# A sliding-window decode layer on one core: its loads on two DMA queues, SyncE's and ScalarE's, and issued one step ahead of use

## The chip, the core and the metric

The kernel runs on one core of a Trainium2 chip. The core has a matrix engine (TensorE, PE in the profile, with weight loads as PEld), a vector engine (VectorE, DVE), a scalar engine (ScalarE, ACT), GpSimd (POOL) and SyncE (SP), which does no arithmetic and here issues DMAs. Sixteen DMA engines move data between HBM and the core's SBUF. Each engine runs its own instructions in program order; engines wait for each other through semaphores. A DMA is issued by an instruction of SP, ACT or POOL and goes into the issuing engine's own queue; an issue that must wait for a buffer holds back what stands behind it on that engine.

The metric is the device time of one execution in microseconds (us), as a median over runs.

## The reference

For two sequences with one new token each, the layer normalises x, and adds to x an attention over a window of the cache and a gated feed-forward part, both computed from the normalised xn. All data are float32.

```python
xn = layernorm(x)                                 # x: (2, 1, 512)
# attention: 32 query heads, 8 key heads, head size 128, the last W = 4096 of 32768 keys
q = (xn @ wq).reshape(2, 1, 32, 128)              # wq: (512, 4096)
k = repeat(k_cache[:, :, Sk - W:, :], 4, axis=1)  # four query heads share a key head
v = repeat(v_cache[:, :, Sk - W:, :], 4, axis=1)
p = softmax(q . k * 128 ** -0.5)
attn = (p . v).reshape(2, 1, 4096) @ wo           # wo: (4096, 512)
# feed-forward: F = 1792
gate = xn @ W_gate
up = xn @ W_up
glu = ((gate * (gate > 0)) * up) @ W_down
return x + attn + glu
```

Each input element is used once or for four heads, so the work is mostly that of bringing 94.9 MB from HBM into SBUF.

## The kernel before, in words

**Groups and tiles.** The 2 x 8 pairs of sequence and key head are cut into four groups g of four key heads of one sequence (`g` = 2r + b, with r the half of the heads and b the sequence). A group's keys come as two tiles, a = 0 and 1, of two heads each, its values likewise. `load_kv` (line 85) loads such a tile: 128 partitions x 8192 floats, 4096 KB, with 32 KB in a row per partition. In this document k(g,a) and v(g,a) are these tiles.

**The ring.** All large loads go through one pool of four buffers, `ring` (`RING = 4`): in this order wq in two halves (`load_wq`, line 75), w_gate and w_up (`load_ff`, line 79), k(0,0), k(0,1), then k(1,0), v(0,0), k(1,1), v(0,1), and so on, a tile of K of group g and one of V of group g-1 in turn up to k(3,1), v(2,1), then v(3,0), v(3,1), w_down (`load_down`, line 82) and wo in two halves, wo0 and wo1, the second in five pieces (line 434). The n-th tile takes the buffer of tile n-4, so its load waits until that tile's last reader is done: a K tile is freed by DVE's second transpose of it, a V tile by PE's last product with it, a weight by PE's last product. All these loads are issued by SP (`nc.sync.dma_start`, line 71) in the order above. The small x is loaded from ACT's queue (line 105).

**The order of the work** is written out by hand (`manual_schedule`): each engine runs its instructions in the order in which the program names them.

- Start: the statistics of x, xn and its transpose; q = xn @ wq into `q_ps` (line 195), 64 matmuls, of which the first 32 read the first half of wq; then `load_ff` twice; the transposes of q (`qt`) and copies of it into `qz` by DVE and ACT (line 217); then `g_ps` and `u_ps` (line 225) from w_gate and w_up, and h.
- `keys(g, a, ...)` (line 242): for each half of the tile, DVE transposes it (line 249, `kT`) and PE adds 16 products to the scores `s` (line 254). After either half it runs a list of `steps`, work of the group before that is put there by hand.
- `softmax(g)` (line 263): maxima on DVE and PE, then the exponentials on ACT (line 286). `turn(g)` (line 290): DVE transposes the result and copies it into `pts` (lines 292, 298).
- `values(g, a, v)` (line 310): 32 matmuls of `pts` with the V tile (line 317).
- `join(g, a)` (line 366): `mask` on DVE (line 326) and `gather` on PE (line 337), after a = 1 also the sums. `close(g)` (line 372): `finish` on DVE, and after each second group `spread_heads` (line 352), PE products whose result ACT copies into `oT` (line 360).

The loop over groups runs like this, with the joins of group g-1 put into the steps of the following `keys`:

```python
for g in range(1, NG):
    for a in range(NP):
        kt_in = load_kv(k_cache, "k", g, a)
        v_in = load_kv(v_cache, "v", g - 1, a)
        keys(g, a, kt_in, steps)
        if a:
            softmax(g)
        values(g - 1, a, v_in)
        if a:
            turn(g)
```

At the end come `values` and `join` of group 3, the product of h with w_down, `spread_heads(1)`, and the products of `oT` with wo (line 415, `yw_ps`; the last four chunks at line 419), one copy each by ACT and DVE and the store of the result.

Of the kernel before, what the change touches and what calls it, by code (L numbers as in the profile page):

```python
# [20 lines left out]
def kernel(  # L21
# [12 lines left out]
    nc = tc.nc  # L34
    P = 128
    B, _, D = x.shape
    _, HKV, SK, DH = k_cache.shape
    HQ = wq.shape[1] // DH
    REP = HQ // HKV
    F = w_gate.shape[1]  # L40
    W = min(4096, max(256, SK // 4))
    KC = D // P
# [6 lines left out]
    NG = B * R  # L49
    S1 = W // (Q * 512)  # L50

    NP = C // 2
# [13 lines left out]
    ctx.enter_context(tc.manual_schedule())  # L66


    def load(name, src, shape):
        t = ring.tile(shape, F32, name=name, tag="ring")  # L70
        nc.sync.dma_start(t, src)
        return t


    def load_wq(m):
        src = wq[m * 2 * P:(m + 1) * 2 * P, :].rearrange("(p k) f -> p k f", p=P)
        return load(f"wq{m}", src, [P, 2, HQ * DH])

    def load_ff(w, name):
        return load(name, w.rearrange("(p k) f -> p k f", p=P), [P, KC, F])  # L80

    def load_down():
        return load("wd", w_down.rearrange("(p k) e -> p k e", p=P), [P, FB, D])

    def load_kv(cache, name, g, a):
        r, b = divmod(g, B)
        base = cache[b, r * C + 2 * a, SK - W:SK, :]
        run = J * DH
        src = bass.AP(
            tensor=cache.tensor, offset=base.offset, ap=[[run, PK], [SK * DH, 2], [1, run]]  # L90
        )
        return load(f"{name}{g}_{a}", src, [P, run])


    NJ = HQ * DH // (R * P)
# [8 lines left out]
    x2 = const.tile([B, D], F32, name="x2")  # L104
    nc.scalar.dma_start(x2, x[:, 0, :])
    wqt = [load_wq(m) for m in range(2)]

    ident = const.tile([P, P], F32, name="ident")
# [68 lines left out]
    for kc in range(KC):  # L177
        m, k = divmod(kc, 2)
# [12 lines left out]
    for kc in range(KC):  # L191
        for r in range(R):
            for c in range(C):
# [2 lines left out]
                    q_ps[r][32 * c:32 * c + 32, :], xnT[:, 0, kc, :], wqt[kc // 2][:, kc % 2, n * 512:(n + 1) * 512],  # L196
                    start=(kc == 0), stop=(kc == KC - 1),
                )
    gw = load_ff(w_gate, "wg")
    uw = load_ff(w_up, "wu")  # L200
    for r in range(R):
        qs = work.tile([P, 512], F32, name=f"qs{r}", tag="qs")
        (nc.vector.tensor_copy if r else nc.scalar.copy)(qs, q_ps[r])  # L203
# [5 lines left out]
        for m in range(NB):  # L209
            src = qt[32 * m:32 * m + 32, :, :, 0].rearrange("p i (t h) b -> p b t h i", h=2)  # L210
# [31 lines left out]
    def keys(g, a, kt_in, steps=((), ())):  # L242

        if a == 0:
            ss[g] = ps_s.tile([P, 512], F32, name=f"s{g}", tag="s")
        for mh in range(2):
            kt = ktp.tile([P, J, 2, 32], F32, name=f"kT{g}_{a}_{mh}", tag="kT")
            src = kt_in.rearrange("p (j d) -> p j d", d=DH)[:, :, PK * mh:PK * mh + PK]
            nc.vector.transpose(kt.rearrange("p j m i -> p j (m i)"), src)  # L249
            for m in range(2):  # L250
                for h in range(2):
                    for s1 in range(S1):
                        q = 2 * h + s1
                        nc.tensor.matmul(  # L254
                            ss[g][32 * q:32 * q + 32, :], qz[:, g, 2 * mh + m, a, h], kt[:, JS * s1:JS * s1 + JS, m, h::2],
                            start=(a == 0 and mh == 0 and m == 0), stop=(a == NP - 1 and mh == 1 and m == 1),
                        )
            for step in steps[mh]:
                step()
# [3 lines left out]
    def softmax(g):  # L263

        m = work.tile([P, 1], F32, name=f"m{g}", tag="m")
        nc.vector.tensor_reduce(out=m, in_=ss[g], op=ALU.max, axis=AX.X)  # L266
        mt = ps_1.tile([1, P], F32, name=f"mt{g}", tag="misc")
        nc.tensor.transpose(mt, m, ident)
        mx = work.tile([1, 2, TK], F32, name=f"mx{g}", tag="mx")
        nc.vector.tensor_reduce(  # L270
            out=mx, in_=mt.rearrange("p (h x k) -> p h k x", h=2, k=TK), op=ALU.max, axis=AX.X
        )
        mb = work.tile([1, 2, S1 * Q, TK], F32, name=f"mb{g}", tag="mb")
        nc.vector.tensor_scalar(
            mb, mx[:, :, None, :].to_broadcast([1, 2, S1 * Q, TK]), -SCALE, None, op0=ALU.mult
        )
        nm_ps = ps_1.tile([P, 1], F32, name=f"nm_ps{g}", tag="misc")
        nc.tensor.matmul(nm_ps, mb.rearrange("p h x k -> p (h x k)"), ones, start=True, stop=True)
        nm = work.tile([P, 1], F32, name=f"nm{g}", tag="nm")
        nc.vector.tensor_copy(nm, nm_ps)  # L280

        l = ls[g] = work.tile([P, 1], F32, name=f"l{g}", tag="l")
        pv = pz.rearrange("p j (i h) -> p j i h", h=2)
        for h in range(2):
            o = slice(PK * h, PK * h + PK)
            nc.scalar.activation(  # L286
                pv[o, :, :, h], ss[g][o].rearrange("p (j i) -> p j i", j=JS), AF.Exp, bias=nm[o], scale=SCALE, accum_out=l[o],
            )

    def turn(g):  # L290
        pT = work.tile([P, JS, Q, NP, REP], F32, name=f"pT{g}", tag="pT", bufs=1)
        nc.vector.transpose(pT.rearrange("p j x t k -> p (j x t k)"), pz.rearrange("p j s -> p (j s)"))  # L292
        pts[g] = work.tile([P, NP, S1, JS, 2, REP], F32, name=f"pt{g}", tag="pt")
        for h in range(2):
            for s1 in range(S1):
                q = 32 * (2 * h + s1)
                for x in range(Q):
                    nc.vector.tensor_copy(  # L298
                        pts[g][32 * x:32 * x + 32, :, s1, :, h], pT[q:q + 32, :, x].rearrange("p j t k -> p t j k")
                    )  # L300
# [3 lines left out]
    def total(g):  # L304
        lps[g] = ps_1.tile([HR, 1], F32, name=f"lp{g}", tag="misc")
        nc.tensor.matmul(lps[g], by_h.rearrange("p t h k -> p (t h k)"), ls[g], start=True, stop=True)
# [3 lines left out]
    def values(g, a, v):  # L310
        o = os[a] = ps_1.tile([P, 512], F32, name=f"o{g}_{a}", tag=f"o{a}")
        for s1 in range(S1):
            for jh in range(2):
                for q in range(Q):
                    j = 16 * jh + 4 * q
                    lo = (JS * s1 + j) * P
                    nc.tensor.matmul(  # L317
                        o[32 * q:32 * q + 32, :],
                        pts[g][:, a, s1, j:j + 4].rearrange("p u h k -> p (u h k)"), v[:, lo:lo + 512],
                        start=(s1 == 0 and jh == 0), stop=(s1 == S1 - 1 and jh == 1),  # L320
                    )

    def mask(g, a):
        o = os[a]
        ons[a] = work.tile([P, 4, P], F32, name=f"on{g}_{a}", tag="on")
        nc.vector.tensor_tensor(  # L326
            ons[a], o.rearrange("p (u d) -> p u d", u=4), own_u[:, :, None].to_broadcast([P, 4, P]), op=ALU.mult
        )
# [4 lines left out]
    def gather(g, a):  # L333

        if a == 0:
            oa[g] = ps_1.tile([HR, 4, P], F32, name=f"oa{g}", tag="oa")
        nc.tensor.matmul(  # L337
            oa[g].rearrange("h u d -> h (u d)"), pick[:, 8 - 8 * a:24 - 8 * a],
            ons[a].rearrange("p u d -> p (u d)"), start=(a == 0), stop=(a == NP - 1),
        )  # L340
# [11 lines left out]
    def spread_heads(r):  # L352
# [6 lines left out]
            )  # L359
        nc.scalar.copy(oT[:, r], op)  # L360

    for a in range(NP):
        keys(0, a, load_kv(k_cache, "k", 0, a))
    softmax(0)
    turn(0)
    def join(g, a):
        mask(g, a)
        gather(g, a)
        if a:
            total(g)  # L370

    def close(g):
        finish(g)
        if g % B == B - 1:
            spread_heads(g // B)

    steps = ((), ())
    for g in range(1, NG):
        for a in range(NP):
            kt_in = load_kv(k_cache, "k", g, a)  # L380
            v_in = load_kv(v_cache, "v", g - 1, a)
            keys(g, a, kt_in, steps)
            if a:
                softmax(g)
            values(g - 1, a, v_in)
            if a:
                turn(g)
            steps = (
                (lambda g=g, a=a: join(g - 1, a),), (lambda g=g: close(g - 1),) if a else (),
            )  # L390
    for step in steps[0] + steps[1]:
        step()
    g = NG - 1
    vin = [load_kv(v_cache, "v", g, a) for a in range(NP)]
    dw = load_down()


# [25 lines left out]
    for a in range(NP):  # L423
        values(g, a, vin[a])
        join(g, a)
# [52 lines left out]
```

## Time and profile before

| | us |
|---|---|
| median of 3 runs | 230.38 |
| lowest and highest run | 230.38 and 230.39 |
| the profiled execution, its own time | 230.5 |
| its span (first to last instruction) | 228.5 |
| PE busy | 132.5 |
| DVE busy | 118.6 |
| ACT busy | 14.2 |

Times in the profile count from the start of the span. A line of a timeline gives the start, the length, the engine, the line of the kernel, the operation, out<-in by the tiles' names, the shapes and, after an x, how many instructions it merges; in square brackets stands the idle time of the engine ahead of it and who ended that. A line of the chain of waits gives a start, a length and who was at work. SPq and ACTq are the issues of DMAs; names leave out the numbers of tiles, so that which K tile a row means follows from the order. The row of digits called DMA cuts the span into 40 equal slices and gives the busy share of the 16 DMA engines in tenths.

### The profile page before, as it was taken

Reading aid. Unit: us, or ns where it says so; the run is one execution under the profiler, and the core shown is the slowest. Engines: PE = TensorE matmul, PEld = TensorE weight load, DVE = VectorE, ACT = ScalarE, POOL = GpSimd, SP = SyncE. Lnnn points to the kernel's source line nnn. Section 1 sums busy time; section 2 is a strip of 40 time slices with the busy share of each in tenths; the row PEclk is TensorE's granted clock in tenths of the full one; section 3 lists DMA queues with packets and bytes.
Section 4 is the critical chain, followed back from the end, with each engine's and each line's share of the span. In section 5 each row is a group of like instructions: output and inputs, shape, how many; then the busy total and the mean of one; then the engine's idle time right before and its main releaser. Section 6 shows DMA issues by size and latency. Waiting matters only on the chain.

```text
span 228.5 us, 2062 instructions
## 1 busy us (share of the span) xinstructions
PE 132.5 (58%) x864; PEld 38.7 (17%) x864; DVE 118.6 (52%) x160; ACT 14.2 (6%) x40; POOL 3.7 (2%) x11
## 2 busy tenths in 40 slices
PE   0584929603636005876906975508928735989693
PEld 0521203101001001211201311102401201223211
DVE  2300032319893399972599893799179295012000
ACT  2000022000000400000200000200000200000001
POOL 6000000000000000000000000000000000000000
PEclk9999575985897655897775899956997995599679
DMA  7999999999999999999999999999999999999991
GB/s 276 459 402 418 467 412 416 453 459 401 430 453 424 403 453 453 393 436 459 419 413 453 433 396 453 445 419 424 453 413 419 453 439 389 461 446 410 412 380 38
DMA packets 3916, 95.03 MB, mean 416 GB/s; under 512 B 442, under 2 KB 450, under 8 KB 836
## 3 DMA queue, kind: packets, MB, share of 16 engines
q1 hardware_dynamic: 3896, 94.90, 97.0%
q8 instruction: 7, 0.11, 0.2%
q10 hardware_dynamic: 12, 0.01, 0.0%
q14 instruction: 1, 0.01, 0.0%
HBM read 94.90 MB, written 0.00 MB: 415 GB/s over the span
## 4 chain that ended last, share of the span: by engine, by line
DMA 60%; DVE 20%; PE 14%; issue 3%; ACT 2%; SPq 0%; DVEq 0%; ACTq 0%
DMA k<-in_A_k_cache_dram 37%; DVE kT L249 15%; DMA wo<-in_A_wo_dram 13%; DMA wq<-in_A_wq_dram 9%; PE yw_ps L415 4%; PE s L254 3%; PE o L317 3%; PE q_ps L195 3%; DVE pt L298 2%; DVE on L326 1%; ACT pz L286 1%; DVE m L266 1%; ACT L286 1%; DVE pT L292 1%; PE y_ps L419 0%
## 5 line engine op out<-in xcount | busy, mean ns | idle before, releaser
L254 PE MATMUL s<-kT,qz 128*32 128x512 f32 x256 | 44.2, 815 | 58.4 <-DVE kT L249 58.4
L249 DVE STREAM_TRANSPOSE kT<-k 128x4096 f32<-128x4096 f32 x16 | 70.6, 4429 | 12.8 <-DMA k<-in_A_k_cache_dram 12.8
L317 PE MATMUL o<-v,pt 128*32 128x512 f32 x256 | 34.5, 672 | 0.0
L254 PEld LDWEIGHTS s<-kT,qz 128*32 128x32 f32 x256 | 8.7, 128 | 86.8 <-issue 61.9
L298 DVE COPY pt<-pT 32x256 f32<-32x256 f32 x64 | 18.2, 285 | 1.0
L195 PE MATMUL q_ps<-wq,xnT 128*32 128x512 f32 x64 | 12.9, 980 | 4.3 <-DMA wq<-in_A_wq_dram 4.3
L217 DVE COPY qz<-qt 32x32 f32<-32x32 f32 x16 | 3.0, 188 | 22.5 <-ACT qz L217 22.5
L337 PE MATMUL oa<-on,pick 128*16 128x512 f32 x16 | 10.1, 721 | 6.9 <-DVE on L326 6.9
L317 PEld LDWEIGHTS o<-v,pt 128*32 128x32 f32 x256 | 9.4, 121 | 19.4 <-issue 19.3
L326 DVE TENSOR_TENSOR on<-o,own_u 128x512 f32<-128x512 f32 x8 | 5.4, 672 | 12.8 <-PE o L317 12.8
L286 ACT ACTIVATE pz<-s,nm 64x512 f32<-64x512 f32 x8 | 5.8, 731 | 80.7 <-DVE nm L280 80.6
L415 PE MATMUL yw_ps<-wo,oT 128*2 128x512 f32 x56 | 8.6, 783 | 2.2 <-DMA wo<-in_A_wo_dram 2.2
L292 DVE STREAM_TRANSPOSE pT<-pz 128x1024 f32<-128x1024 f32 x4 | 5.0, 1245 | 8.3 <-ACT pz L286 8.3
L446 DVE COPY yo<-y_ps 128x128 f32<-128x128 f32 x1 | 0.3, 292 | 16.9 <-PE y_ps L419 16.9
L266 DVE TENSOR_REDUCE m<-s 128x1 f32<-128x512 f32 x4 | 2.8, 692 | 11.5 <-PE s L254 11.5
L183 PE MATMUL xt_ps<-rep,xc 2*128 2x32 f32 x16 | 3.7, 402 | 8.4 <-DVE rep L176 8.4
L195 PEld LDWEIGHTS q_ps<-wq,xnT 128*32 128x32 f32 x64 | 3.0, 168 | 13.1 <-issue 7.7
L225 PE MATMUL g_ps<-wg,xnT 128*32 128x448 f32 x32 | 5.0, 791 | 0.0
L183 PEld LDWEIGHTS xt_ps<-rep,xc 2*128 2x128 f32 x16 | 3.6, 319 | 8.4 <-DVE rep L176 8.4
L206 PE MATMUL qt<-ident,qs 128*128 128x128 f32 x8 | 1.7, 357 | 4.4 <-DVE qs L203 4.4
L337 PEld LDWEIGHTS oa<-on,pick 128*16 128x16 f32 x16 | 1.6, 113 | 15.2 <-DVE on L326 9.8
L355 PEld LDWEIGHTS op<-osb,spread 16*128 16x128 f32 x32 | 3.7, 186 | 1.8 <-issue 1.8
(68 smaller groups left out, 53.9 us busy)
## 6 DMA issues: line engine op xcount, KB each, us to landing
k<-in_A_k_cache_dram SPq DMA_DIRECT2D x8, 4096.0 KB, 29.4
v<-in_A_v_cache_dram SPq DMA_DIRECT2D x8, 4096.0 KB, 28.5
wq<-in_A_wq_dram SPq DMA_DIRECT2D x2, 4096.0 KB, 16.8
wo<-in_A_wo_dram SPq DMA_DIRECT2D x1, 4096.0 KB, 30.1
wg<-in_B_W_gate_dram SPq DMA_DIRECT2D x1, 3584.0 KB, 29.5
wu<-in_B_W_up_dram SPq DMA_DIRECT2D x1, 3584.0 KB
wd<-in_B_W_down_dram SPq DMA_DIRECT2D x1, 3584.0 KB
wo<-in_A_wo_dram SPq DMA_DIRECT2D x1, 2048.0 KB, 19.5
```

What stands on the lines that cost most here:

```text
L183: nc.tensor.matmul(xt_ps[:, v, kc, :], lhsT, rep16.rearrange("r s b -> r (s b)"), start=True, stop=True)
L195: nc.tensor.matmul(q_ps[r][32 * c:32 * c + 32, :], xnT[:, 0, kc, :], wqt[kc // 2][:, kc % 2, n * 512:(n + 1) * 512], start=(kc == 0), stop ...
L249: nc.vector.transpose(kt.rearrange("p j m i -> p j (m i)"), src)
L254: nc.tensor.matmul(ss[g][32 * q:32 * q + 32, :], qz[:, g, 2 * mh + m, a, h], kt[:, JS * s1:JS * s1 + JS, m, h::2], start=(a == 0 and mh == ...
L266: nc.vector.tensor_reduce(out=m, in_=ss[g], op=ALU.max, axis=AX.X)
L286: nc.scalar.activation(pv[o, :, :, h], ss[g][o].rearrange("p (j i) -> p j i", j=JS), AF.Exp, bias=nm[o], scale=SCALE, accum_out=l[o],)
L292: nc.vector.transpose(pT.rearrange("p j x t k -> p (j x t k)"), pz.rearrange("p j s -> p (j s)"))
L298: nc.vector.tensor_copy(pts[g][32 * x:32 * x + 32, :, s1, :, h], pT[q:q + 32, :, x].rearrange("p j t k -> p t j k"))
L317: nc.tensor.matmul(o[32 * q:32 * q + 32, :], pts[g][:, a, s1, j:j + 4].rearrange("p u h k -> p (u h k)"), v[:, lo:lo + 512], start=(s1 == ...
L326: nc.vector.tensor_tensor(ons[a], o.rearrange("p (u d) -> p u d", u=4), own_u[:, :, None].to_broadcast([P, 4, P]), op=ALU.mult)
L337: nc.tensor.matmul(oa[g].rearrange("h u d -> h (u d)"), pick[:, 8 - 8 * a:24 - 8 * a], ons[a].rearrange("p u d -> p (u d)"), start=(a == 0 ...
L415: nc.tensor.matmul(yw_ps[32 * c:32 * c + B, :], lhsT, w, start=(n < Q), stop=(n >= wide - Q))
```

## The change

Loads get a queue. SP keeps the first half of wq, w_gate, all K tiles, v(3,0), v(3,1), w_down and wo. ACT gets the second half of wq, w_up and the V tiles of groups 0, 1 and 2. The loop now issues the tiles of the next step after it has named the keys of this one, so that the issues on ACT stand at given places among its other work: v(0,0) ahead of softmax(0), v(g-1,1) after keys(g,0), v(g,0) ahead of softmax(g). The order in which tiles take the ring's buffers is as before.

```diff
-    def load(name, src, shape):
+    def load(name, src, shape, queue=nc.sync):
         t = ring.tile(shape, F32, name=name, tag="ring")
-        nc.sync.dma_start(t, src)
+        queue.dma_start(t, src)
         return t
...
-        return load(f"wq{m}", src, [P, 2, HQ * DH])
+        return load(f"wq{m}", src, [P, 2, HQ * DH], nc.scalar if m else nc.sync)
...
-    gw = load_ff(w_gate, "wg")
-    uw = load_ff(w_up, "wu")
+    gw = load_ff(w_gate, "wg", nc.sync)
+    uw = load_ff(w_up, "wu", nc.scalar)
...
+    def load_k(g, a):
+        return load_kv(k_cache, "k", g, a)
+
+    def load_v(g, a):
+        return load_kv(v_cache, "v", g, a, nc.scalar if g < NG - 1 else nc.sync)
+
     for a in range(NP):
-        keys(0, a, load_kv(k_cache, "k", 0, a))
+        kt_in = load_k(0, a)
+        keys(0, a, kt_in)
+    k_next = load_k(1, 0)
+    v_next = load_v(0, 0)
     softmax(0)
     turn(0)
...
     for g in range(1, NG):
         for a in range(NP):
-            kt_in = load_kv(k_cache, "k", g, a)
-            v_in = load_kv(v_cache, "v", g - 1, a)
+            kt_in, v_in = k_next, v_next
             keys(g, a, kt_in, steps)
-            if a:
+            if a == 0:
+                k_next = load_k(g, 1)
+                v_next = load_v(g - 1, 1)
+            else:
+                if g < NG - 1:
+                    k_next = load_k(g + 1, 0)
+                v_next = load_v(g, 0)
                 softmax(g)
             values(g - 1, a, v_in)
...
-    vin = [load_kv(v_cache, "v", g, a) for a in range(NP)]
+    vin = [v_next, load_v(g, 1)]
     dw = load_down()
```

More of the change, by code (lines that the diff above doesn't have):

```diff
@@ L76, in load_wq, with load_ff, load_kv @@
         src = wq[m * 2 * P:(m + 1) * 2 * P, :].rearrange("(p k) f -> p k f", p=P)
-        return load(f"wq{m}", src, [P, 2, HQ * DH])
-    def load_ff(w, name):
-        return load(name, w.rearrange("(p k) f -> p k f", p=P), [P, KC, F])
+        return load(f"wq{m}", src, [P, 2, HQ * DH], nc.scalar if m else nc.sync)
+    def load_ff(w, name, queue):
+        return load(name, w.rearrange("(p k) f -> p k f", p=P), [P, KC, F], queue)
     def load_down():
         return load("wd", w_down.rearrange("(p k) e -> p k e", p=P), [P, FB, D])
-    def load_kv(cache, name, g, a):
+    def load_kv(cache, name, g, a, queue=nc.sync):
         r, b = divmod(g, B)
@@ L91, in load_kv @@
         )
-        return load(f"{name}{g}_{a}", src, [P, run])
+        return load(f"{name}{g}_{a}", src, [P, run], queue)
     NJ = HQ * DH // (R * P)
```

## The prediction

> **What bounds the kernel now.** I read the page first, then the chain of waits, then the timelines of SP, DVE, ACT and PE. A tile of group g and pair a is written k(g,a) or v(g,a).
>
> ```profile
> span 228.5 us, 2062 instructions
> ...
> DMA  7999999999999999999999999999999999999991
> ...
> q1 hardware_dynamic: 3896, 94.90, 97.0%
> ```
>
> One queue moves 94.90 MB, its packets fill 97.0% of the span on the 16 DMA engines, and the busy digit is 9 in every slice but the first and the last. The transfers are the bound; compute matters only where it frees a ring buffer too late. The chain of waits in order of time gives the pace:
>
> ```profile
> 29.35 30.88 DMA k<-in_A_k_cache_dram
> ...
> 103.67 24.96 DMA k<-in_A_k_cache_dram
> ...
> 138.06 29.27 DMA k<-in_A_k_cache_dram
> ...
> 184.72 30.11 DMA wo<-in_A_wo_dram
> ```
>
> A row starts at an issue or at the last wait before it, and ends at the landing: k(0,1) at 60.23, k(2,1) at 128.63, k(3,1) at 167.33, wo0 at 214.83. k(3,1), issued at 138.06, took 29.27 us: three tiles are in flight at a time. From the first to the second there are seven tiles, k(1,0), v(0,0), k(1,1), v(0,1), k(2,0), v(1,0), k(2,1): 68.40 / 7 = 9.77 us each (a tile is 128 x 8192 x 4 bytes, 4.194 MB). The next four take 38.70 / 4 = 9.68. The stream runs without a hole from 60 to 215, so v(0,1), fourth after k(0,1), landed at about 60.23 + 4 x 9.77 = 99.3.
>
> How near is a hole? The timeline of SP's issues:
>
> ```profile
> 44.12 0.54 SPq L71 DMA_DIRECT2D v<-in_A_v_cache_dram  x1
> ...
> 92.67 0.53 SPq L71 DMA_DIRECT2D k<-in_A_k_cache_dram  x1
> 98.59 0.54 SPq L71 DMA_DIRECT2D v<-in_A_v_cache_dram  x1
> ...
> 145.93 0.54 SPq L71 DMA_DIRECT2D v<-in_A_v_cache_dram  x1
> ...
> 159.74 8.19 SPq L71 DMA_DIRECT2D v<-in_A_v_cache_dram  x2
> ```
>
> These are v(0,0) at 44.12, k(2,0) at 92.67, v(1,0) at 98.59, then v(2,1) at 145.93, and v(3,0) and v(3,1) from 159.74 on, the second at 167.4. At 92.67 only v(0,1) is still in flight, with 6.6 us left. This is the thinnest place of the stream. How long a transfer takes that starts into an empty queue is shown by the tile view of wq:
>
> ```profile
> DMA to landing us min/median/max: 12.2/16.8/21.4
> ```
>
> The first wq half needs 12.2 us where a tile in the flow needs 9.77, so an issue must come some 2.4 us before the flow runs dry. The margin at k(2,0) is therefore 6.6 - 2.4 = 4.2 us.
>
> **The change part by part.** Bytes, tiles, the order of the ring's four buffers and which reader frees which buffer stay the same; "one step ahead" alters program order only, and SP already issued a tile as soon as its buffer was free. The eight issues that leave SP save it eight times about 0.5 us that the stream covers: nothing. ACT gets them; an issue of 0.54 us there lies in an engine that is idle for tens of us between softmaxes. A waiting issue holds back what stands behind it on ACT: v(g,0) stands ahead of the exponentials of group g and waits for values(g-1,0), but on PE those end before keys(g,1), on which the exponentials wait anyway. Nothing there. Two other effects do cost.
>
> First: two transfers of different queues are now in flight together, and nothing orders them. At the start wq0 and wq1 share the engines and land together, and so do w_gate and w_up. The timelines of PE and DVE:
>
> ```profile
> 13.09 6.27 PE L195 MATMUL q_ps<-wq,xnT 128*32 128x512 f32 x32 [1.02 <-DMA wq<-in_A_wq_dram]
> 22.68 6.60 PE L195 MATMUL q_ps<-wq,xnT 128*32 128x512 f32 x32 [3.32 <-DMA wq<-in_A_wq_dram]
> ...
> 35.23 5.02 PE L225 MATMUL g_ps<-wg,xnT 128*32 128x448 f32 x32
> 40.84 3.21 PE L225 MATMUL u_ps<-wu,xnT 128*32 128x448 f32 x32 [0.58 <-DMA wu<-in_B_W_up_dram]
> ...
> 181.02 3.64 PE L317 MATMUL o<-v,pt 128*32 128x512 f32 x32
> ...
> 214.87 8.63 PE L415 MATMUL yw_ps<-wo,oT 128*2 128x512 f32 x56 [2.23 <-DMA wo<-in_A_wo_dram]
> ```
>
> ```profile
> 50.54 8.77 DVE L249 STREAM_TRANSPOSE kT<-k 128x4096 f32<-128x4096 f32 x2 [4.83 <-DMA k<-in_A_k_cache_dram]
> 60.35 8.77 DVE L249 STREAM_TRANSPOSE kT<-k 128x4096 f32<-128x4096 f32 x2 [1.04 <-DMA k<-in_A_k_cache_dram]
> ...
> 167.35 4.45 DVE L249 STREAM_TRANSPOSE kT<-k 128x4096 f32<-128x4096 f32 x1 [6.71 <-DMA k<-in_A_k_cache_dram]
> ...
> 189.13 0.69 DVE L326 TENSOR_TENSOR on<-o,own_u 128x512 f32<-128x512 f32 x1
> ```
>
> The first half of q's products, hidden under the second half's load so far, now starts only when both have landed, at 22.7. All 64 end at 22.7 + 6.3 + 6.6 = 35.6, 6.3 later. The steps from there to g_ps keep their 5.9 us: g_ps at 41.5, u_ps at 46.5, its end at 49.7. w_gate and w_up are there by then (15.7 MB, 40.8 as before), and k(0,0) and k(0,1), issued at about 29 and 36, wait behind them: no hole, k(0,0) at 50.5 as before. But v(0,0) goes out at 49.7 beside k(0,1), where one queue had put it two tiles behind. Its flow starts, in terms of landings, at 49.7 + 2.4 = 52.1; k(0,1) would land at 60.2 and has 8.1 us to go. If the two share equally, these take twice as long: **k(0,1) lands 8.1 us later**, at 68.3. Bounds: nothing if SP's queue is served first, 9.77 if all of v(0,0) goes first. The trace of before has no two large transfers on two queues, so I take the middle, equal shares, as both consist of the same packets.
>
> The Trainium skill, "DMA: Bandwidth & Descriptors", section "Queues, rings and completion order", says that each DMA engine serves its queues in turn, a packet at a time; by it the 8.1 would stand. No run so far shows it.
>
> DVE is idle ahead of both pairs of transposes, so keys(0,1), softmax(0), keys(1,0) and with them the issue of k(2,0) move by the same 8.1, to 100.8. v(0,1) also goes out later, as on ACT it stands behind the exponentials of group 0, but k(1,0) and k(1,1), issued long before, cover it.
>
> The stream, whose bytes are the same, still runs dry at 99.3 with v(0,1). Delay less margin: 8.1 - 4.2 = **a hole of 3.9 us**. A byte lost there is not made up, so everything in the stream moves by 3.9: wo0 from 214.83 to 218.7. Later issues move by 8.1 against a flow later by 3.9, and there the margins hold. The nearest is k(2,1): k(2,0) issued at 100.8 has about 4 us left when v(1,0) joins it at 109.1; sharing brings k(2,0) in at 117, v(1,0) at 129 and k(2,1) at 136.4, and DVE, which by the chain of waits took it as it landed, comes to it at 128.63 + 8.1 = 136.7. At k(3,1) DVE had waited 6.71 us. There compute catches up: k(3,1) lands at 171.2, and DVE, ready at 168.7, is from then on 3.9 late, not 8.1.
>
> Second: v(2,1). ACT's timeline has the copy that now stands ahead of it, and the last one of its kind:
>
> ```profile
> 163.80 0.18 ACT L360 COPY oT<-op 128x32 f32<-128x32 f32 x1 [19.56 <-PE op L355]
> ...
> 212.68 0.18 ACT L360 COPY oT<-op 128x32 f32<-128x32 f32 x1 [29.65 <-PE op L355]
> ```
>
> Its buffer is free at 145.93, but on ACT it stands behind the copy of oT, which ends at 163.98, 172.1 with the delay. So v(2,1), until now ahead of v(3,0), comes behind it or beside it. v(3,0) is out at 167.8 and alone would land at 181.0; v(2,1) joins at 174.5, so both run at half pace until v(3,0) lands at 187.5; the 3.3 us left of v(2,1) take 6.6 beside v(3,1): 194.1. values(2,1), 3.64 us in the row at 181.02, ends at 197.7; the mask behind it, at 189.13 before, is **8.6 late**, and so is all of PE's work for group 3 up to the last oT copy. That copy had been done at 212.86, 2.0 ahead of wo0; now 221.4, 2.7 behind it. The last projection starts at 221.4 instead of 214.87, 6.6 later.
>
> Some of this comes back: wo1's pieces are then there, and the 56 matmuls that took 8.63 ran at 3.12 for 24 where nothing held them:
>
> ```profile
> 219.09 3.12 PE L415 MATMUL yw_ps<-wo,oT 128*2 128x512 f32 x24
> ```
>
> That is 7.3 for 56, 1.3 less. So +6.6 at most, +3.9 (the stream) at least. I take 6.6 - 1.3 = +5.3: 230.5 of the profiled execution (its span is 228.5) becomes 235.8. The median of the runs is 0.1 below the profiled execution: **235.7 us**.
>
> **The rivals.**
>
> *No hole* (22%). If the engines serve the queues in the order of issue, or SP's first, k(0,1) is not late by more than the 4.2 margin and the flow never breaks. v(2,1) then lands one tile late, behind v(3,0), at 187; the mask would come some 2 us late, the last oT copy at about wo0's landing: 230.4, no change. For it speaks that all bytes are the same and the bound is the bytes.
>
> The Trainium skill, same page, section "Issuing engines are not separate DMA queues", says that issuing from several engines saves only the issue time; read alone, it gives this rival's 230.4. The trace agrees that issue is cheap (0.54 us).
>
> *A larger hole* (13%). If ACT's queue gets more than half wherever both wait, V, which nobody needs yet, delays K. k(0,1) is then up to 9.77 late, the hole 5.6, and k(2,1) misses DVE by some us, as its margin by the sum above is 0.3: stream +5.6 to +7, with PE's tail +1 to +3 on it, 237 to 240.
>
> *Faster* (10%). The flow itself gets quicker with two queues: 22.6 tiles' worth of bytes at 9.68 instead of 9.77 is 2.0 us, and the start, where k(0,0) lands at 50.5 though 4.75 tiles' worth of bytes at 9.77 is 46.4, has 4.1 us of which 2.4 + 0.7 are the first issue and latency: 1.0 could go. Together -3.0: 227.4. It needs every packet slot of the engines to gain, and it decides only if k(2,0) is still issued before the flow ends, thus if k(0,1) is late by under 4.2 us. Against it: 97.0% of the span is packets already.
>
> The Trainium skill, same page, section "Specifications", gives a fabric ceiling of 435 GB/s; 4.194 MB in 9.77 us is 429, so by the page at most 1.3% of pace is left.
>
> **How the numbers follow.** The forecast has 55%: the order of events rests on rows, equal sharing does not. Slower by more than 0.2% (about what a measurement of this kernel can tell from no change) holds the forecast and the larger hole, 0.68; within 0.2% is the rival without a hole, 0.22; faster 0.10. The likeliest case alone spans 233.0 to 238.0: the stream's 3.9 less an uncertain 1.3 in the margin, up to the tail's 6.6 and 1 more. The range for all, 230.1 to 239.5, takes in the case without a hole and most of the larger hole; it leaves out the faster case and the top of the larger hole.
>
> **What would show it.** Right: k(0,1)'s first transpose near 68 instead of 60.35; u_ps ending near 50; the issue of k(2,0) at about 101, and a DMA digit under 9 in the slice around 99 to 103, the 18th; ACT issuing v(2,1) right behind the oT copy and PE waiting for v before the last values of group 2; the last projection starting on oT and not on wo. Wrong: k(0,1) still at 60 (the queues don't share), all slices at 9 (no hole), or a pace away from 9.7 us a tile.

## The result and the profile after

The changed kernel takes 238.08 us (median of 4 runs, 236.51 to 240.01), the kernel before 230.38: a ratio of 1.0334, 95% interval 1.0253 to 1.0416. It is slower by 7.7 us, the loss is larger than forecast, and the changed kernel's runs lie 3.5 us apart where those of before lie 0.3 apart. The profiled execution took 238.74 us. A run more than 1.5% above the fastest of its kernel enters no ratio; that leaves out two of v_act's four runs, 240.86 and 249.61 us.

The page of the changed kernel, the same lines as before and the second queue:

```profile
span 236.9 us, 2061 instructions
...
DMA  7999999999999999379999999999999999999980
...
q1 hardware_dynamic: 2744, 61.87, 61.8%
q10 hardware_dynamic: 1164, 33.04, 32.4%
```

94.9 MB as before, now 61.87 on SP's queue and 33.04 on ACT's. The row of digits shows one break: 3 and 7 in slices 17 and 18, which begins at 16 x 236.9 / 40 = 95 us. Finer windows of the same kernel (start:end, length, busy time and count of PE, PEld, DVE, ACT and POOL, granted clock, DMA share, GB/s):

```profile
94.00:96.00 2.00, 0.00 (x0) 0.00 (x0) 2.00 (x1) 0.00 (x0) 0.00 (x0) 0.50 0.95 410
96.00:98.00 2.00, 0.88 (x8) 0.28 (x11) 2.00 (x2) 0.00 (x0) 0.00 (x0) 0.50 0.35 147
98.00:100.00 2.00, 2.00 (x16) 0.39 (x8) 2.00 (x1) 0.00 (x0) 0.00 (x0) 0.50 0.04 8
100.00:102.00 2.00, 1.41 (x8) 0.20 (x8) 2.00 (x2) 0.00 (x0) 0.00 (x0) 0.50 0.00 0
102.00:104.00 2.00, 2.00 (x20) 0.53 (x16) 2.00 (x1) 0.00 (x0) 0.00 (x0) 0.77 0.91 262
...
168.00:170.00 2.00, 1.47 (x15) 0.37 (x14) 2.00 (x3) 0.00 (x0) 0.00 (x0) 1.00 0.95 410
170.00:172.00 2.00, 2.00 (x21) 0.79 (x13) 0.33 (x2) 0.00 (x0) 0.00 (x0) 1.00 0.81 295
172.00:174.00 2.00, 2.00 (x21) 1.61 (x24) 0.59 (x1) 0.19 (x1) 0.00 (x0) 1.00 0.93 279
174.00:176.00 2.00, 2.00 (x24) 0.56 (x20) 2.00 (x1) 0.00 (x0) 0.00 (x0) 1.00 0.91 295
176.00:178.00 2.00, 1.09 (x16) 0.18 (x12) 2.00 (x2) 0.00 (x0) 0.00 (x0) 1.00 1.07 442
```

The reader sees a hole and a dip. From 96 to 104 us 417 x 2 = 834 KB came in; the flow of one tile in 9.77 us, 429 GB/s, would have brought 3432. The difference is worth 6.1 us. From 170 to 176 it is 1738 KB instead of 2574: 2.0 us. Together 8.1 of the 8.4 us by which the span grew. (By the windows the flow ends near 97; by the landings I had put that at 99.3.)

Where the hole comes from is read from single rows of the timelines of PE, ACT, DVE and SP in the order of time:

```profile
20.35 9.06 PE L195 MATMUL q_ps<-wq,xnT 128*32 128x512 f32 x64 [8.28 <-DMA wq<-in_A_wq_dram]
...
37.68 5.07 PE L225 MATMUL g_ps<-wg,xnT 128*32 128x448 f32 x32 [2.48 <-DMA wg<-in_B_W_gate_dram]
43.61 3.21 PE L225 MATMUL u_ps<-wu,xnT 128*32 128x448 f32 x32 [0.86 <-DMA wu<-in_B_W_up_dram]
```

```profile
46.89 0.63 ACTq L71 DMA_DIRECT2D v<-in_A_v_cache_dram  x1
```

```profile
50.71 8.77 DVE L249 STREAM_TRANSPOSE kT<-k 128x4096 f32<-128x4096 f32 x2 [2.23 <-DMA k<-in_A_k_cache_dram]
70.24 8.77 DVE L249 STREAM_TRANSPOSE kT<-k 128x4096 f32<-128x4096 f32 x2 [10.76 <-DMA k<-in_A_k_cache_dram]
```

```profile
101.33 0.53 SPq L71 DMA_DIRECT2D k<-in_A_k_cache_dram  x1
```

All of q's products run only after the first half of wq lands at 20, and yet end at 29.41, where before they ended at 29.28. What comes late is w_gate and w_up: PE waits 2.48 us for the one and 0.86 for the other, which is there at 43.6 instead of 40.8. The products with w_up end at 46.82 and free the buffer of v(0,0), which is out at 46.89; k(0,0) lands where it did, but DVE waits 10.76 us for k(0,1), which comes at 70.2 instead of 60.2; and k(2,0) is issued at 101.33 instead of 92.67, when the flow is dry.

How the two queues shared while k(0,1) and v(0,0) were both under way is told by what each moved from 50 to 60 us (packets, MB, share of the 16 engines' time; q1 is SP's queue, q10 ACT's):

```profile
q1 hardware_dynamic: 71, 2.29, 53.3%
q10 hardware_dynamic: 64, 2.10, 48.7%
```

The shares are nearly equal. Had all of v(0,0) gone first, k(0,1) would have been as late, 9.77 us, but SP's queue would have moved next to nothing in this stretch.

The end of the chain of waits:

```profile
173.47 24.62 DMA v<-in_A_v_cache_dram
...
198.13 5.54 PE o L317 x32
...
212.66 20.46 DMA wo<-in_A_wo_dram
```

v(2,1) is issued right behind the oT copy, at 173.47, and lands at 198.09; PE waits for it before values(2,1). The last piece of wo lands at 233.12 and the kernel ends 3.8 us later.

### The profile page after: what moved, and what is told of

The parts are those of the page before. It is cut to its first block, busy times and chain, and to the rows that moved or that the text cites. A ratio compares the mean times of both kernels' runs of the same rounds, so it can differ in the third digit from the quotient of the medians.

```text
span 236.9 us, 2061 instructions
## 1 busy us (share of the span) xinstructions
PE 124.0 (52%) x864; PEld 37.2 (16%) x864; DVE 118.5 (50%) x160; ACT 14.1 (6%) x40; POOL 3.7 (2%) x11
## 3 DMA queue, kind: packets, MB, share of 16 engines
q1 hardware_dynamic: 2744, 61.87, 61.8%
q10 hardware_dynamic: 1164, 33.04, 32.4%
## 4 chain that ended last, share of the span: by engine, by line
DMA 29%; DVE 18%; PE 11%; issue 1%; SPq 1%; ACT 0%; ACTq 0%
DVE kT L249 13%; DMA v<-in_A_v_cache_dram 10%; DMA k<-in_A_k_cache_dram 10%; DMA wo<-in_A_wo_dram 9%; PE o L317 5%; PE s L254 3%; DVE pt L298 2%; DVE on L326 1%; PE op L355 1%; SPq L449 1%; DVE pT L292 1%; ACT pz L286 0%; PE oa L337 0%; DVE m L266 0%; DVE od L349 0%
## 5 line engine op out<-in xcount | busy, mean ns | idle before, releaser
L254 PE MATMUL s<-kT,qz 128*32 128x512 f32 x256 | 43.0, 800 | 62.0 <-DVE kT L249 62.0
L195 PE MATMUL q_ps<-wq,xnT 128*32 128x512 f32 x64 | 9.1, 729 | 8.3 <-DMA wq<-in_A_wq_dram 8.3
L337 PE MATMUL oa<-on,pick 128*16 128x512 f32 x16 | 8.2, 594 | 2.5 <-DVE on L326 2.5
L430 PE MATMUL yw_ps<-wo,oT 128*2 128x512 f32 x56 | 6.6, 592 | 1.8 <-DMA wo<-in_A_wo_dram 1.7
L195 PEld LDWEIGHTS q_ps<-wq,xnT 128*32 128x32 f32 x64 | 2.5, 131 | 14.1 <-issue 14.1
L355 PE MATMUL op<-osb,spread 16*128 16x32 f32 x32 | 3.9, 273 | 0.0
## 6 DMA issues: line engine op xcount, KB each, us to landing
wq<-in_A_wq_dram SPq DMA_DIRECT2D x1, 4096.0 KB, 19.5
```

The costliest lines, as they stand in the source:

```text
L195: nc.tensor.matmul(q_ps[r][32 * c:32 * c + 32, :], xnT[:, 0, kc, :], wqt[kc // 2][:, kc % 2, n * 512:(n + 1) * 512], start=(kc == 0), stop ...
L254: nc.tensor.matmul(ss[g][32 * q:32 * q + 32, :], qz[:, g, 2 * mh + m, a, h], kt[:, JS * s1:JS * s1 + JS, m, h::2], start=(a == 0 and mh == ...
L337: nc.tensor.matmul(oa[g].rearrange("h u d -> h (u d)"), pick[:, 8 - 8 * a:24 - 8 * a], ons[a].rearrange("p u d -> p (u d)"), start=(a == 0 ...
L355: nc.tensor.matmul(op, spread.rearrange("h k e -> h (k e)")[:, NE - 1 - e:NE - 1 - e + P], osb[r][:, :, e * NJ:(e + 1) * NJ].rearrange("h ...
L430: nc.tensor.matmul(yw_ps[32 * c:32 * c + B, :], lhsT, w, start=(n < Q), stop=(n >= wide - Q))
```

## The experiments

The theory after the result: the bytes' flow is the bound, and it breaks where a tile of V on the second queue takes half of the engines from a tile of K that DVE waits for; K late by more than a few us means that the next buffer is freed after the flow has run dry. The rivals: (A) the new program order costs; (B) two queues slow the flow by themselves; (C) the halves of wq, landing together, delay everything; (D) the late v(2,1) costs nothing of its own; (E) each us of lateness costs one, without a margin. Each run was timed beside the kernel before on the same chip, whose medians there were 230.37 to 230.43; a ratio stands with its 95% interval.

**order_only**: everything on SP, in the program order of the change.

```diff
-        return load(f"wq{m}", src, [P, 2, HQ * DH], nc.scalar if m else nc.sync)
+        return load(f"wq{m}", src, [P, 2, HQ * DH], nc.sync)
...
-    uw = load_ff(w_up, "wu", nc.scalar)
+    uw = load_ff(w_up, "wu", nc.sync)
...
-        return load_kv(v_cache, "v", g, a, nc.scalar if g < NG - 1 else nc.sync)
+        return load_kv(v_cache, "v", g, a, nc.sync)
```

> All loads are on SP's queue, the program order is that of the change. Theory (the loss is made by transfers of two queues that share the engines while K is wanted: k(0,1) lands late, k(2,0) is issued after the flow has run dry, and v(2,1) stands behind the oT copy on ACT): as before, 230.4 us, within 0.5. Rival A (the new program order itself, one step ahead, costs): 233 or more.

Measured 230.4 us, ratio 0.9999 (0.9990 to 1.0008). "One step ahead" neither gains nor costs; rival A is out.

**weights_act**: only the last of these three edits; wq and w_up stay split, V is on SP.

> Only the second half of wq and w_up are on ACT's queue; all of V is on SP. Theory: q comes a few us later, but k(0,0) still lands at about 50.5 and k(0,1) at 60.2, no hole: 230.4 us, within 0.7. Rival A: 233 or more. Rival B (two large transfers at once slow the flow itself, wherever they meet): the 15.7 MB of weights land later than 40.9 us and the end moves by as much, 1 us or more.

Measured 230.5 us, ratio 1.0003 (0.9990 to 1.0015). DVE's timeline of this run:

```profile
50.57 8.77 DVE L249 STREAM_TRANSPOSE kT<-k 128x4096 f32<-128x4096 f32 x2 [3.64 <-DMA k<-in_A_k_cache_dram]
60.39 8.77 DVE L249 STREAM_TRANSPOSE kT<-k 128x4096 f32<-128x4096 f32 x2 [1.05 <-DMA k<-in_A_k_cache_dram]
```

Both K tiles land as before. 15.7 MB over two queues at once cost the flow nothing that can be measured: two large transfers together are not slow in themselves, so rival B is out for the weights.

**v_act**: the first two edits alone; the weights on SP, V on ACT.

> The weights are on SP, V of groups 0 to 2 on ACT. Theory: v(0,0), out at 44.1, shares with k(0,0) and k(0,1); k(0,1) lands at about 70 instead of 60.2, a hole of 5 to 6 us ahead of k(2,0), v(2,1) late as in the changed kernel: 236 to 240 us. Rival C (the halves of wq landing together cause the delay): under 233.

Ratio 1.0324 (1.0278 to 1.0371), from two runs, thus about 237.9 us; the loss of the whole change. Its first transposes of k(0,1) start at 70.12, and it has the same hole. Rival C is out: V is enough.

**one_queue_late_k**: the kernel before, all on SP, but v(0,0) issued ahead of k(0,1) and k(1,0). Buffers are taken in the old order; only the issues change places.

```diff
-    for a in range(NP):
-        keys(0, a, load_kv(k_cache, "k", 0, a))
+    keys(0, 0, load_kv(k_cache, "k", 0, 0))
+    later = []
+    k01 = load_kv(k_cache, "k", 0, 1, later)   # takes the buffer, no DMA yet
+    k10 = load_kv(k_cache, "k", 1, 0, later)
+    v00 = load_kv(v_cache, "v", 0, 0)
+    for t, src in later:
+        nc.sync.dma_start(t, src)
+    keys(0, 1, k01)
```

> The kernel before, one queue, with v(0,0) issued ahead of k(0,1) and k(1,0); the buffers are taken in the old order. k(0,1) then lands 9.8 us later, with no second queue at all. Theory (lateness of k(0,1) beyond a margin of 4.2 us opens a hole): k(0,1) at 70.0, a hole of about 5.6 us ahead of k(2,0), the end 5.6 later, 236 us (235 to 237.5). Rival B (the second queue slows the flow): no more than 231.

Measured 236.46 us, ratio 1.0279 (1.0237 to 1.0321). Its DVE timeline and windows:

```profile
70.34 8.77 DVE L252 STREAM_TRANSPOSE kT<-k 128x4096 f32<-128x4096 f32 x2 [10.74 <-DMA k<-in_A_k_cache_dram]
```

```profile
96.00:98.00 2.00, 0.76 (x4) 0.23 (x8) 2.00 (x2) 0.00 (x0) 0.00 (x0) 0.50 0.42 180
98.00:100.00 2.00, 2.00 (x16) 0.43 (x8) 2.00 (x1) 0.00 (x0) 0.00 (x0) 0.50 0.04 8
100.00:102.00 2.00, 1.41 (x8) 0.20 (x8) 2.00 (x2) 0.00 (x0) 0.00 (x0) 0.50 0.00 0
102.00:104.00 2.00, 2.00 (x20) 0.59 (x16) 2.00 (x1) 0.00 (x0) 0.00 (x0) 0.85 0.85 262
```

This is the hole of the changed kernel, almost number by number, without any second queue. So about 6.1 us of the loss is the price of k(0,1) at 70 instead of 60, whatever makes it late.

**late_half, late_quarter, late_three_quarters, split_only**: the same kernel with only a part of v(0,0) ahead of k(0,1), CUT of its 8192 columns, and the rest in the old place; in split_only both parts are in the old place.

```diff
-    v00 = load_kv(v_cache, "v", 0, 0)
+    v00 = ring.tile([P, J * DH], F32, name="v0_0", tag="ring")
+    nc.sync.dma_start(v00[:, 0:CUT], part(v_cache, 0, 0, 0, CUT))
     for t, src in later:
         nc.sync.dma_start(t, src)
+    nc.sync.dma_start(v00[:, CUT:J * DH], part(v_cache, 0, 0, CUT, J * DH))
```

> The kernel before, one queue, with half of v(0,0) issued ahead of k(0,1) and the other half in its old place: k(0,1) lands 4.9 us later. Theory with its margin of 4.2 us: a hole of 0.7 us, 231.1 (230.6 to 231.8). Rival E (every us by which K is late costs one): 235.

> The kernel before, one queue, with a quarter of v(0,0) issued ahead of k(0,1): k(0,1) lands 2.45 us later. The whole tile cost 6.1 us for 9.8 of lateness, half of it 1.25 for 4.9: a margin of 3.7 us in both. Theory: 2.45 is under the margin, no hole, 230.4 us (within 0.5). Rival E (lateness costs in proportion, 6.1 / 9.8 of it): 231.9.

> The kernel before, one queue, v(0,0) loaded by two DMAs, a quarter and three quarters of it, both behind k(1,0): the cut of the quarter's run without its lateness. If the cut is free, 230.4 us (within 0.4), and the 1.1 us of the quarter's run are the price of lateness 2.45; if the cut or its shorter packets cost, 231 to 231.6, and lateness 2.45 is free.

> The kernel before, one queue, three quarters of v(0,0) ahead of k(0,1): lateness 7.35 us. With a margin of 3.7, as the whole and the half tile gave, a hole of 3.6: 234.0 us (233.3 to 234.8). In proportion to lateness from nothing (rival E): 6.1 x 0.75 = 4.6, 235.0.

| part of v(0,0) ahead | k(0,1) late by (worked out) | median us | ratio, 95% interval |
|---|---|---|---|
| none, tile cut (split_only) | 0 | 230.51 | 1.0006 (0.9997 to 1.0015) |
| a quarter | 2.45 | 231.51 | 1.0038 (1.0007 to 1.0069) |
| half | 4.9 | 231.68 | 1.0071 (1.0038 to 1.0104) |
| three quarters | 7.35 | 233.94 | 1.0170 (1.0145 to 1.0195) |
| all | 9.8 | 236.46 | 1.0279 (1.0237 to 1.0321) |

From half on each further 2.45 us cost 2.3 and 2.5: about one for one, beyond a margin of 3.7 by the medians (whole tile: 9.8 - 6.1; half: 4.9 - 1.25). Three quarters came out where that margin puts it (234.0 forecast), and half and three quarters both lie below proportion (233.5 and 235.0): rival E is out. The quarter missed: it should have been free and cost 1.1, its runs lying between 230.3 and 233.1; taken alone it would fit proportion (231.9). The half's eight runs lie in two groups, five from 231.4 to 231.7 and three from 233.3 to 234.1. The cut itself is free.

Not all of the 3.7 us is a margin of the flow. Between k(0,1) and the issue of k(2,0) stand the last 16 products of keys(0,1) on PE, shown here by one row of each, for the kernel before, the changed one, the quarter and the whole tile (L257 is the same line of these longer files):

```profile
69.18 3.30 PE L254 MATMUL s<-kT,qz 128*32 128x512 f32 x16 [2.23 <-DVE kT L249]
79.07 2.04 PE L254 MATMUL s<-kT,qz 128*32 128x512 f32 x16 [0.69 <-DVE kT L249]
71.59 3.64 PE L257 MATMUL s<-kT,qz 128*32 128x512 f32 x16 [0.69 <-DVE kT L252]
79.17 2.08 PE L257 MATMUL s<-kT,qz 128*32 128x512 f32 x16 [0.69 <-DVE kT L252]
```

The granted clock was 0.50 (70 to 72), 1.00 (79 to 82), 0.55 (71 to 76) and 1.00 (79 to 82). So with the whole tile ahead k(0,1) begins 10.0 us late, but k(2,0) is out at 101.45, only 8.8 late, and 5.9 are missing (450 x 2 = 900 KB instead of 3432): at the issue of k(2,0) the margin is 2.9. In the quarter's profiled execution, 232.57 us, k(0,1) begins 2.4 late and k(2,0) is out 2.8 late, at 95.44. That uses up the whole margin; that other runs of the quarter lie on the free side of it would explain their spread, but only one of them was profiled. From 94 to 102 that execution has:

```profile
94.00:96.00 2.00, 1.41 (x11) 0.20 (x8) 2.00 (x2) 0.00 (x0) 0.00 (x0) 0.50 0.89 369
96.00:98.00 2.00, 2.00 (x24) 0.59 (x20) 2.00 (x1) 0.00 (x0) 0.00 (x0) 1.00 0.92 360
98.00:100.00 2.00, 2.00 (x24) 0.67 (x20) 1.74 (x1) 0.00 (x0) 0.00 (x0) 1.00 0.97 344
100.00:102.00 2.00, 2.00 (x24) 0.70 (x20) 0.77 (x2) 0.00 (x0) 0.00 (x0) 1.00 0.96 377
```

No hole, but 1450 x 2 = 2900 KB where the flow brings 3432: 1.2 us short. By the margin of 2.9, 2.8 late should have cost next to nothing. That the 16 engines run dry one after the other, and not all at once, would explain the rest; no view used here shows single engines, so this is argued, not shown.

**v00_late**: the changed kernel with v(0,0) issued behind the exponentials of group 0.

```diff
-    v_next = load_v(0, 0)
     softmax(0)
+    v_next = load_v(0, 0)
     turn(0)
```

> The changed kernel with one line moved: v(0,0) is issued behind the exponentials of group 0 on ACT instead of ahead of them, at about 78 us instead of 47. Both queues stay in use. Theory: k(0,1) lands at 60.2 again, k(2,0) is out at about 93, no hole; v(2,1) still stands behind the oT copy, but lands behind v(3,0) by about 187 to 190, which brings the last oT copy to about wo0's landing: 230.4 to 231.2 us. Rival B (the second queue slows the flow itself): 235 or more.

Measured 233.43 us, ratio 1.0130 (1.0093 to 1.0167): one line gives back 4.7 of the 7.7 us, but not all, where at most 231.2 us was expected; rival B's 235 or more did not come either. The first hole is gone; there is another. DVE's timeline and windows of this run:

```profile
60.47 8.77 DVE L249 STREAM_TRANSPOSE kT<-k 128x4096 f32<-128x4096 f32 x2 [1.03 <-DMA k<-in_A_k_cache_dram]
...
135.28 4.45 DVE L249 STREAM_TRANSPOSE kT<-k 128x4096 f32<-128x4096 f32 x1 [8.40 <-DMA k<-in_A_k_cache_dram]
```

```profile
164.00:168.00 4.00, 4.00 (x24) 0.99 (x20) 3.33 (x4) 0.00 (x0) 0.00 (x0) 0.65 0.74 262
168.00:172.00 4.00, 4.00 (x40) 2.38 (x36) 2.42 (x1) 0.19 (x1) 0.00 (x0) 1.00 0.76 311
```

k(0,1) and k(2,0) are in time again, but k(2,1), which shares with v(1,0) and v(1,1), lands at 135.3 instead of 128.6, and DVE waits 8.4 us for it. Then v(3,0) is out at 166.33 (159.74 before) and v(2,1), behind the oT copy, at 170.69: the flow is short by (2 x 429 - 573) x 4 = 1140 KB, 2.7 us. The profiled execution, 234.73 us, is 4.2 longer than that of before; the rest is not traced. The expectation had overlooked this second late K.

**oT_dve**: the changed kernel, the oT copy on DVE.

```diff
-        nc.scalar.copy(oT[:, r], op)
+        nc.vector.tensor_copy(oT[:, r], op)
```

> The changed kernel with only the copy of oT moved to DVE. The first hole stays (k(0,1) at 70, k(2,0) issued at 101); v(2,1) is out at about 155 to 158 instead of 173, the second dip of the stream at 170 to 176 goes, and PE no longer waits 11 us for v(2,1). Theory: the two losses are separate, 6.1 and 2.0 us of stream: 236 us (235 to 237). Rival D (v(2,1) costs nothing of its own): as the changed kernel, 238.

Measured 238.53 us, ratio 1.0335 (1.0293 to 1.0376): no gain, the expectation failed. v(2,1) is out at 159.60 instead of 173.47 and the dip at 170 to 176 has gone, but the chain of waits of this run has

```profile
148.56 33.00 DMA k<-in_A_k_cache_dram
...
226.65 6.16 PE yw_ps L430 x56
```

k(3,1) lands at 181.56 instead of 173.4, now with v(2,1) under way beside it. The last projection starts at 226.65 without any wait for wo; PE, not the flow, now ends last. But the profiled execution, at 239.46 us the slowest of the four, also has a new dip, and its hole is larger:

```profile
84.00:92.00 8.00, 0.55 (x2) 0.50 (x2) 4.10 (x12) 2.85 (x5) 0.00 (x0) 0.50 0.87 353
96.00:106.00 10.00, 6.36 (x40) 1.55 (x44) 10.00 (x3) 0.00 (x0) 0.00 (x0) 0.60 0.41 152
```

Against 429 GB/s, 1.4 and 6.5 us are missing, 7.9 together, about as much as the 8.1 of the changed kernel, which from 96 to 106 lacks 5.8 by the same count. v(0,1), behind the exponentials on ACT, is out at 86.83 there instead of 84.90. So this run does not tell what v(2,1) costs by itself, and rival D, which had the time right, is left to the next runs.

**v00_late_oT_dve**: both edits.

> As the run with v(0,0) behind the exponentials, and the copy of oT is made by DVE instead of ACT, so that v(2,1) waits for its buffer alone (free at about 146). Theory: 230.4 us, within 0.5, the time of the kernel before. Rival B: 235 or more.

Measured 232.39 us, ratio 1.0074 (1.0042 to 1.0106), 1.7 us slower than before by the ratio and 2.0 by the medians, where none was expected. No hole is left, only a dip of about 0.6 us (393 GB/s from 76 to 82, where the kernel before has 433); k(3,1) needs 30.80 us and DVE begins it at 175.08 (167.35 before), and the last projection starts at 219.29 (214.87 before) with wo there. So an early v(2,1) costs too, through k(3,1), which it runs beside.

**v00_late_v21_sync**: v(0,0) late, v(2,1) on SP behind k(3,1); the other five V tiles, half of wq and w_up stay on ACT.

```diff
-        return load_kv(v_cache, "v", g, a, nc.scalar if g < NG - 1 else nc.sync)
+        return load_kv(v_cache, "v", g, a, nc.scalar if 2 * g + a < 2 * NG - 3 else nc.sync)
```

> The changed kernel with v(0,0) issued behind the exponentials of group 0, and v(2,1) on SP behind k(3,1). Five tiles of V stay on ACT's queue. Theory as it now stands (the second queue costs only where a tile of V takes the engines from a tile of K that DVE waits for, or where ACT issues late): k(2,1) is late as in the run with v(0,0) alone moved, near 135, but v(2,1) neither takes from k(3,1) nor waits for the oT copy: k(3,1) near 169, v(2,1) near 179, no hole, 230.4 to 231.4 us. Rival B (each tile on the second queue slows the flow): 232.4 or more, as with the oT copy on DVE.

Measured 231.43 us, ratio 1.0046 (1.0027 to 1.0065), at the upper edge of what was expected. DVE's timeline:

```profile
135.11 4.45 DVE L249 STREAM_TRANSPOSE kT<-k 128x4096 f32<-128x4096 f32 x1 [7.64 <-DMA k<-in_A_k_cache_dram]
...
169.33 4.45 DVE L249 STREAM_TRANSPOSE kT<-k 128x4096 f32<-128x4096 f32 x1 [2.24 <-DMA k<-in_A_k_cache_dram]
```

k(2,1) near 135 and k(3,1) near 169, as said. Seven of the eight large loads that the change gave to ACT are still there, and 6.6 of the 7.7 us are back. From v00_late only the queue of v(2,1) differs, and 2.0 us (233.43 to 231.43) are back: a late v(2,1) has a cost of its own, and rival D is out. About 1 us stays. Most of it may be a dip, for which the windows of this run and, below it, of the kernel before are:

```profile
76.00:82.00 6.00, 0.00 (x0) 0.00 (x0) 5.05 (x15) 0.70 (x2) 0.00 (x0) 0.50 0.98 382
76.00:82.00 6.00, 0.00 (x0) 0.00 (x0) 4.04 (x11) 1.73 (x5) 0.00 (x0) 0.54 1.01 433
```

It is worth 0.7 us and stands where v(0,0) and v(0,1), out at 75.17 and 75.90, join the flow. Why it is there, and what makes up the rest, is open, and with it whether rival B holds for V by some tenths of a us. No version was faster than the kernel before.

## Why the prediction was right in kind and too small, point by point

- *Bound and place.* Right. The flow was the bound, its thinnest place was k(2,0), and it broke there; 8.1 of the span's 8.4 us are missing flow.
- *Nothing from the order and the issues.* Right: order_only, 0.9999.
- *The start.* v(0,0) was to be late, and was, but not by the step forecast. That step was q's products, ending at 35.6. The halves of wq did not land together: products began at 20.35, and 64 of them took 9.06 us, where I had taken 22.7 and the 12.9 us of before's two rows; the second of these ran at a granted clock of 0.50 (windows 22 to 28 of before), while in the changed kernel it was 1.00 up to 34. So q cost nothing (29.41). What made v(0,0) late the prediction had put at nothing, with "w_gate and w_up are there by then" and 40.8 as before: w_gate, sharing with w_up, came at 37.7, and w_up at 43.6, beside bytes of k(0,0), which was out on SP's queue at 26.04 and ran there once w_gate was in (from 38 to 42 SP's queue moved 1.21 MB, ACT's 0.46). So v(0,0) went out at 46.89, 2.8 later than before, not at 49.7.
- *Equal shares.* They held. v(0,0), out 2.8 us earlier, was beside k(0,1) for the whole of it: 50.5 + 2 x 9.77 = 70.0, and DVE began at 70.24. The term of 8.1 became 9.9. The Trainium skill, "DMA: Bandwidth & Descriptors", section "Queues, rings and completion order", says that each engine serves its queues in turn, packet by packet; this case's trace agrees, with 2.29 and 2.10 MB from the two queues in 10 us, and 19.5 us for a tile beside another instead of 9.77.
- *The hole.* 3.9 was forecast, 6.1 measured. Most of the 2.2 is the margin, the term that was mis-sized: k(2,0) was out 8.7 late (101.33) and 6.1 are missing, so the margin there was 2.6 and not 4.2. It rested on the landing of v(0,1) at 99.3, and from 96 to 98 the flow was already down to 147 GB/s. The other 0.6 is lateness. k(0,1) came 1.8 later than forecast, but PE won back 1.2 of it, as the last 16 products of keys(0,1) took 2.04 us instead of 3.30. That the issue of k(2,0) fell so near its forecast (100.8) is luck: two errors cancelled.
- *k(2,1) and k(3,1).* DVE began k(2,1) at 136.99 (136.4 forecast), k(3,1) at 173.41 (171.2 forecast, plus the 2.2 more of the hole).
- *v(2,1).* Its place behind the oT copy was right (173.47; 172.1 forecast), it landed at 198.09 (194.1). For the places behind k(2,0) the prediction said that the margins hold; at v(3,0) its own numbers leave 171.2 - 167.8 - 2.4 = 1.0 us. A second shortage came there: 2.0 us. This is the term that was missing. A margin taken 1.6 too large, as at k(2,0), would explain it; no run tests that at this place. PE's tail, which I had made the end, was late as forecast (last projection at 223.41; 221.4 forecast), but with 2.0 us more of missing flow wo's last piece ended last.
- *The sum.* The forecast's +5.3 was 3.9 of missing flow and 1.4 of PE's tail beyond it. In the profiled execution, +8.2, the flow lacks 6.1 + 2.0 and the tail adds nothing: 5.3 + 2.2 + 2.0 - 1.4 = 8.1. The median, +7.7, lies 0.5 lower.
- *The rival without a hole* held for weights_act, where the shared bytes were not in K's way. The Trainium skill, "DMA: Bandwidth & Descriptors", section "Issuing engines are not separate DMA queues", says that issuing from several engines saves only the issue time; for the flow of weights_act the ratio of 1.0003 agrees. In the changed kernel the order of arrival changed too, and cost 7.7 us.
- *The rival with a larger hole* (237 to 240) holds the measured time, but not its reason: it needed ACT's queue to get more than half, and k(2,1) to miss DVE by some us. The queues shared evenly, and DVE waited 0.53 us for k(2,1).

## What to carry to other kernels

Where transfers bound a kernel, one queue is also a schedule: it brings the tiles in the order in which they are wanted. Here a load on a second queue took half of the engines at once, also for a tile that nobody needed yet (v(0,0), out at 46.89, is first read at 103.92), and the tile in the critical place took twice as long. Check for each place how late a load may be before the flow runs dry (here 3.7 us of lateness of k(0,1) by the medians, and 2.6 to 2.9 at the issue of k(2,0) itself). If two queues are used, issue the less urgent tile behind an event that comes late enough: one moved line brought back 4.7 of 7.7 us.

## What was not expected of the hardware

Two queues with a large load each shared the engines so evenly that a tile took 19.5 us instead of 9.77, yet 15.7 MB over two queues were as fast as over one (ratio 1.0003). Runs of kernels whose flow comes near a hole or has one spread more: 236.5 to 240.0 us in the changed kernel, but also 230.3 to 233.1 with one queue and a quarter of v(0,0) ahead, against 230.4 to 230.7 before. What the profiles show that could make it is PE's granted clock: the same 16 products ahead of k(2,0)'s issue took 3.64 us at 0.55 and 2.08 at 1.00, in a place where the margin is 2.6 to 2.9 us. Whether it is the whole reason is not shown.
